# One softmax at the kernel's start: maxima subtracted by a second pass of scores on PE instead of by ACT's bias; one step of a weight decode moved by one

## The chip, the cores and the metric

One core of one Trainium2 chip runs the whole program in one launch. The metric is the device time of one execution in microseconds. Engine names: PE (matrix products), DVE, ACT and POOL (element by element), SP (issues DMAs).

## The reference

Three layers run one after the other, all in float32. The attention has 4 sequences of 576 tokens, 8 heads of 64; heads 0–3 see the last 32 tokens, heads 4–7 every 32nd token:

```
scores = scale * (q @ k.T);  scores = where(mask[head], scores, -1e9)
attn = exp(scores - max(scores));  attn = attn / (sum(attn) + 1e-9)
x = attn @ v                                  # 2304 tokens x 512
h = x @ w_in;   x = (h * cos(h)) @ w_out      # 512 -> 2048 -> 512
h = x @ w_in2;  P = a0 + a1*h + a2*h^2 + a3*h^3
Q = 1 + |b0|*|h| + |b1|*h^2;  out = (P / (Q + 1e-6)) @ w_out2
```

Both layers' weights reach the chip as 64-bit floating-point numbers and are made float32 there; the scale is 1/8.

## The kernel before, in words

**Tiling.** A sequence is worked in two halves of 288 tokens, numbered n = 0 to 7 over the four sequences; the two halves of sequence 0 are n = 0 and n = 1. Heads go in four pairs (0, 1 local; 2, 3 strided). For one half and one pair, five blocks of queries have scores against 89 key columns (local) or, in a second half, 126 columns (strided): 445 columns in one PSUM bank, or 378 and 252 columns in two. PSUM has eight banks: two tagged `a`, two `h`, four `y`.

**The float32 products** of the two dense layers are three products of rounded parts each (high·high, high·low, low·high). So every input (`xh`, `xl`, by `att_oe`, L367: ACT makes the high part, DVE the low part), every activation (`gh`, `gl`) and every weight (`wh`, `wl`) is split in two.

**Stages.** `START` (L82), a list written by hand, is run command by command before the first dense step (L813–814). It holds all of the attention of n = 0, and of n = 1 the scores and the softmax up to the sums, while the first weights are decoded. Then come steps g = 0, 1, ... of the first dense layer, each of which works 128 of the 2048 columns of one block of tokens: `l1` (products into `h`, L408), a gate on ACT, DVE and POOL, and some steps later `l2` (products into `y`, L427). Attention of later halves is strewn in between, by tables. The second dense layer follows after 128 such steps.

**The softmax of n = 1** in `START` takes two commands for each pair. `red` (`att_red`, L289) has DVE reduce the scores in PSUM to the maximum of each row and block (L292) and scale it by −1/8 (L293). `exps` (`att_exps`, L296) has ACT do five exponentials, one for each block, with that maximum as bias (L302), and each adds up its row's sum by an accumulator that is read out by an instruction of its own. Two other forms are in the file: `redn` with `ex` (L317–327), which expects that the maximum has been subtracted in PSUM, and `att_s` (L214) called a second time, which writes the scores again into the same banks and adds a product of the unit matrix with the negative maxima (L249–250).

**What sets the order.** The program's order on each engine is the order in which these commands and steps issue it; no scheduler changes it. An engine runs its own queue in order and waits where an input isn't there or a buffer isn't free. Scores of n = 1 lie in the four `y` banks (pairs 0 to 2) and the two `a` banks (pair 3). On DVE, the reductions of `START` are followed by the decode of weights (L154, L156), the reciprocals of the sums (L333, L334) and the gate of step 0 (L499, L507, L511).

**Second weights.** While the first layer runs, the 32 tiles of the second layer's weights are decoded (`plan_w2`, L579) in 16 slots of two tiles. Each slot of `W2ABS` (L80) names five steps: load, g0, g1, g2, g3. In step g0, `first` has ACT make for each tile the magnitude (L143) and the low bits (L147); in g1, `second` calls `dec_ops` with 0, which does nothing; in g2 DVE merges both (L154); in g3 DVE sets the sign (L156) and the tile is stored. A step's order is a string of letters (`C_ORD`, L86): `N` is the sine (L509), `M` the gate's product (L511), `L` runs what the step has planned of this kind.

Of the kernel before, what the change touches and what calls it, by code (L numbers as in the profile page):

```python
# [91 lines left out]
def attention_moe_moe_kernel(ctx: ExitStack, tc: tile.TileContext, qk0, qk, vv, w1, w2, consts, a, b, out):  # L92
# [42 lines left out]
        (eng or SP).dma_start(out=t.rearrange("p n w -> p (n w)"), in_=src[f, o].bitcast(I32))  # L135
        raws[key, f, o] = t

    def dec_abs(key, f, o, eng=None):
        t = raws.pop((key, f, o))
        m = stage("dec")  # L140
        src = t[:, :, 1].bitcast(F32)
        if eng is None:
            ACT.activation(out=m, in_=src, func=AF.Copy, scale=2.0 ** -112)  # L143
        else:
            eng.tensor_scalar(out=m, in0=src, scalar1=2.0 ** -112, scalar2=None, op0=ALU.mult)

# [770 lines left out]
```

## Time and profile before

| | |
|---|---|
| three runs | 977.61, 979.04, 979.51 us (median 979.04) |
| the profiled execution's own time | 975.9 us |
| its span | 974.1 us, granted PE clock 0.987 on average |
| PE busy | 919.2 us (94%) |
| DVE, ACT, POOL busy | 700.5 (72%), 707.9 (73%), 292.5 us (30%) |
| DMA | 91 GB/s over the span |

PE is busy nearly throughout, but not in the first tenth of the span, where attention and weight decode fill it badly. The profiled execution took 1.8 us more than its span and is 3.1 us shorter than the median of the three runs. A busy time is the time in which an engine's instructions run; an idle time in brackets stands ahead of the instruction that ended it, with the instruction that released it.

### The profile page before, as it was taken

The page shows a single profiled execution, that of the slowest core. Times are in us where ns is not written, and L with a number is a line of the kernel's source. Part 1 is how long each engine was busy: PE and PEld are TensorE (multiplying, and loading weights), DVE is VectorE, ACT ScalarE, POOL GpSimd, SP SyncE. Part 2 cuts the span into 40 slices and gives each one's busy share as a digit, 9 for nine tenths or more (in the row PEclk, how much of TensorE's full clock was granted, in tenths as well). Part 3 has the DMA queues.
Part 4 walks back from the last instruction along what each step waited for, and adds up shares of the span by engine and source line. Part 5 has one row for each costly group of instructions (what it writes and reads, how often), then busy time and mean ns, then how long its engine had stood idle before and what let it go on. Part 6 is the DMA issues. An engine that isn't in the chain of part 4 may idle for free.

```text
span 974.1 us, 17268 instructions
## 1 busy us (share of the span) xinstructions
PE 919.2 (94%) x6367; PEld 857.1 (88%) x6367; DVE 700.5 (72%) x1305; ACT 707.9 (73%) x1485; POOL 292.5 (30%) x279
## 2 busy tenths in 40 slices
PE   7678999999999999999899999999999999999997
PEld 6567999998989989899899978888898898898895
DVE  5997754775555575656658797787787787787776
ACT  5987765665775865757758877777777877777875
POOL 2577722142222132221312223223223223232221
PEclk9799999999999999999999999999999999999999
DMA  9766104435335244344226420010100100100000
GB/s 309 265 221 210 45 2 129 152 112 149 114 101 156 93 144 140 130 136 148 91 78 201 128 78 1 8 58 1 40 26 1 66 1 1 66 1 0 34 1 33
DMA packets 51525, 89.35 MB, mean 92 GB/s; under 512 B 4584, under 2 KB 28400, under 8 KB 51440
## 3 DMA queue, kind: packets, MB, share of 16 engines
q1 hardware_dynamic: 50720, 86.58, 27.0%
q10 hardware_dynamic: 720, 1.67, 0.5%
q8 instruction: 50, 0.82, 0.3%
q14 instruction: 35, 0.29, 0.1%
HBM read 70.40 MB, written 17.83 MB: 91 GB/s over the span
## 4 chain that ended last, share of the span: by engine, by line
PE 23%; ACT 22%; DVE 19%; POOL 10%; issue 5%; DMA 1%; POOLq 0%; ACTq 0%; DVEq 0%
PE h L408 10%; POOL z L467 9%; PE y L427 9%; DVE r L470 7%; ACT r L466 6%; ACT r L465 5%; ACT gh L476 4%; DVE h L471 3%; DVE a L471 3%; PE a L363 1%; PE a L248 1%; DVE t L511 1%; PE a L344 1%; ACT dec L143 1%; ACT L509 1%
## 5 line engine op out<-in xcount | busy, mean ns | idle before, releaser
L408 PE MATMUL h<-xh,w 128*128 128x288 f32 (+3 forms) x1408 | 338.6, 312 | 15.5 <-DVE t L511 11.9
L408 PEld LDWEIGHTS h<-xh,w 128*128 128x128 f32 x1408 | 245.1, 191 | 21.7 <-DVE t L511 13.1
L427 PE MATMUL y<-gh,w 128*128 128x288 f32 (+2 forms) x1024 | 229.3, 300 | 0.5 <-ACT w L162 0.5
L408 PE MATMUL h<-xl,w 128*128 128x288 f32 (+3 forms) x704 | 206.8, 310 | 0.0
L427 PE MATMUL y<-w,gh 128*128 128x512 f32 x576 | 195.9, 393 | 5.6 <-DVE ev L441 4.6
L467 POOL TENSOR_TENSOR z<-q,r 128x384 f32<-128x384 f32 x96 | 97.4, 1014 | 297.9 <-ACT r L466 287.8
L427 PEld LDWEIGHTS y<-gh,w 128*128 128x128 f32 x1024 | 172.1, 189 | 0.8 <-ACT w L162 0.8
L427 PE MATMUL y<-gl,w 128*128 128x288 f32 (+2 forms) x512 | 151.7, 296 | 2.2 <-POOL gl L517 2.1
L408 PEld LDWEIGHTS h<-xl,w 128*128 128x128 f32 x704 | 134.7, 191 | 1.8
L427 PEld LDWEIGHTS y<-w,gh 128*128 128x128 f32 x576 | 108.1, 188 | 28.1 <-DVE ev L441 7.1
L517 POOL TENSOR_TENSOR gl<-t,gh 128x288 fp32r<-128x288 f32 (+2 forms) x67 | 68.6, 1025 | 186.9 <-ACT gh L515 162.0
L470 DVE SCALAR_TENSOR_TENSOR r<-z,r 128x384 f32<-128x384 f32 x96 | 69.5, 724 | 74.1 <-POOL z L467 74.1
L427 PE MATMUL y<-w,gl 128*128 128x512 f32 x288 | 114.7, 398 | 5.2 <-DVE gl L481 5.0
L497 ACT ACTIVATE t<-h,biases 128x288 int32<-128x288 f32 (+2 forms) x116 | 57.7, 497 | 78.5 <-PE h L408 66.1
L507 DVE SCALAR_TENSOR_TENSOR u<-h,t 128x288 f32<-128x288 f32 (+2 forms) x128 | 58.2, 455 | 68.5 <-ACT hs L503 53.3
L408 PE MATMUL a<-xh,w 128*128 128x384 f32 x384 | 106.2, 337 | 0.0
L427 PEld LDWEIGHTS y<-gl,w 128*128 128x128 f32 x512 | 97.1, 190 | 3.0 <-POOL gl L517 2.9
L515 ACT ACTIVATE gh<-t 128x288 fp32r<-128x288 f32 (+2 forms) x128 | 56.7, 443 | 27.7 <-DVE t L511 25.6
L509 ACT ACTIVATE u<-u,biases 128x288 f32<-128x288 f32 (+2 forms) x128 | 67.8, 530 | 12.1 <-DVE u L507 11.7
L511 DVE TENSOR_TENSOR t<-u,hs 128x288 f32<-128x288 f32 (+1 forms) x91 | 49.2, 541 | 36.7 <-ACT u L509 36.5
L408 PEld LDWEIGHTS a<-xh,w 128*128 128x128 f32 x384 | 70.5, 188 | 1.8
L427 PEld LDWEIGHTS y<-w,gl 128*128 128x128 f32 x288 | 54.0, 188 | 20.1 <-DVE gl L481 12.1
(113 smaller groups left out, 1612.9 us busy)
## 6 DMA issues: line engine op xcount, KB each, us to landing
raw<-in_w_dram SPq DMA_DIRECT2D x63, 512.0 KB
qk<-in_qk_dram SPq DMA_DIRECT2D x18, 481.0 KB
wf<-dec SPq DMA_DIRECT2D x32, 256.0 KB
wf<-wf SPq DMA_DIRECT2D x32, 256.0 KB
x2s<-x2d SPq DMA_DIRECT2D x24, 192.0 KB
out_dram<-ev SPq DMA_DIRECT2D x17, 256.0 KB
v<-in_vv_dram SPq DMA_DIRECT2D x16, 240.0 KB
v<-in_vv_dram SPq DMA_DIRECT2D x24, 157.5 KB
```

The source lines that it names most:

```text
L408: PE.matmul(h[:, :n], w[d["ph"], f, 0][:, 128 * c:128 * c + 128], x[c][:, cs], start=k == 0, stop=k == len(ops) - 1)
L427: PE.matmul(y, l, r, start=first and i == 0 and bk != bB, stop=last and i == 2 and bk != bA)
L466: ACT.activation(out=r, in_=r, func=AF.Exp, scale=-1.0, bias=biases[:, 1:2])
L467: POOL.tensor_tensor(out=z, in0=q, in1=r, op=ALU.mult)
L470: DVE.scalar_tensor_tensor(out=r, in0=z, scalar=2.0, in1=r, op0=ALU.subtract, op1=ALU.mult, reverse0=True)
L471: DVE.scalar_tensor_tensor(out=h, in0=h, scalar=ab[:, 0:1], in1=r, op0=ALU.add, op1=ALU.mult)
L497: ACT.activation(out=k, in_=h, func=AF.Identity, scale=INV_2PI, bias=biases[:, 2:3])
L507: DVE.scalar_tensor_tensor(out=u, in0=h, scalar=INV_2PI, in1=k, op0=ALU.mult, op1=ALU.subtract)
L509: ACT.activation(out=u, in_=u, func=AF.Sin, scale=TWO_PI, bias=biases[:, 3:4])
L511: DVE.tensor_tensor(out=t, in0=u, in1=e.get("hs", h), op=ALU.mult)
L515: ACT.activation(out=e["gh"], in_=t, func=AF.Copy)
L517: (POOL if c == "H" else DVE).tensor_tensor(out=e["gl"], in0=t, in1=e["gh"].bitcast(F32), op=ALU.subtract)
```

## The change

In `START`, for n = 1: `oe 0 3` (the split of the last outputs of n = 0) stands ahead of the softmax instead of behind the second `red`. `red` becomes `redn`; then `psub` has PE do the whole score pass of that pair a second time into the same banks (mask, scores, and the product of the unit matrix with the negative maxima, 445 or 378 + 252 columns); `ex` is one exponential for each bank; `sum` is a reduction on DVE. For that the tiles of q and k are kept (a flag that was there). In the second weights' decode, the low bits are made in step g1 instead of g0, by a function `dec_low` cut out of `dec_abs`. The tables are untouched; lines behind `dec_abs` are 4 higher in the new file.

```diff
-START = [ ...
-'s 1 3 a', 'red 1 0', 'd 2 1 2', 'red 1 1', 'd 2 0 2', 'exps 1 0', 'oe 0 3', 'split 2 0 POOL', 'exps 1 1',
-'red 1 2', 'split 2 1 POOL', 'd 3 1 0', 'red 1 3', 'exps 1 2', 'exps 1 3', 'd 3 0 0', 'd 3 0 1', 'd 3 1 1',
...
+START = [ ...
+'s 1 3 a', 'oe 0 3', 'redn 1 0', 'psub 1 0', 'd 2 1 2', 'redn 1 1', 'psub 1 1', 'd 2 0 2', 'ex 1 0', 'sum 1 0',
+'split 2 0 POOL', 'ex 1 1', 'sum 1 1', 'redn 1 2', 'psub 1 2', 'split 2 1 POOL', 'd 3 1 0', 'redn 1 3', 'psub 1 3',
+'ex 1 2', 'sum 1 2', 'ex 1 3', 'sum 1 3', 'd 3 0 0', 'd 3 0 1', 'd 3 1 1',
...
+    def dec_low(t):
+        src = t.rearrange("p n w -> p (n w)").bitcast(U8).rearrange("p (n b) -> p n b", b=8)[:, :, 3]
+        ACT.activation(out=t[:, :, 0], in_=src, func=AF.Copy, scale=1.0 / 32.0, bias=-31.0 / 64.0)
...
-    def dec_abs(key, f, o, eng=None):
+    def dec_abs(key, f, o, eng=None, low=True):
...
-        ACT.activation(out=t[:, :, 0], in_=t.rearrange("p n w -> p (n w)").bitcast(U8).rearrange("p (n b) -> p n b", b=8)[:, :, 3],
-                       func=AF.Copy, scale=1.0 / 32.0, bias=-31.0 / 64.0)
+        if low:
+            dec_low(t)
...
             def first(f=f):
-                raws["m", f] = [dec_abs(2, f, o) for o in range(2)]
+                raws["m", f] = [dec_abs(2, f, o, low=False) for o in range(2)]
...
             def second(f=f, c=0):
                 for t, m in raws["m", f]:
-                    dec_ops(c, t, m)
+                    dec_ops(c, t, m) if c else dec_low(t)
```

On PE, at the end of `START`, the row of before goes from the last scores of n = 1 (pair 3, in the `a` banks) straight to the first products of step 0 (L408):

```order
L237 MATMUL a<-cst_78 128x378
L245 MATMUL a<-k_249,qk 64x126 x6
L237 LDWEIGHTS cst_78
L237 MATMUL a<-cst_78 128x252
L245 MATMUL a<-k_249,qk 64x126 x4
L408 MATMUL h<-xh_84,w_403 128x256
L408 MATMUL h<-xl_88,w_403 128x256
L408 MATMUL h<-xh_85,w_403 128x256
L408 MATMUL h<-xl_89,w_403 128x256
```

Now, behind those scores, the same pass stands once more for each pair, with a product of `mx` at each bank's end, and only then the products of step 0 (L412 now). The rows are those of pair 3's second pass; 16 rows of the same kind, for pairs 0 to 2, stand ahead of them:

```order
L241 LDWEIGHTS cst_78
L241 MATMUL a<-cst_78 128x378
L249 MATMUL a<-k_249,qk 64x126 x6
L254 MATMUL a<-mx,cst 128x378
L241 LDWEIGHTS cst_78
L241 MATMUL a<-cst_78 128x252
L249 MATMUL a<-k_249,qk 64x126 x4
L254 MATMUL a<-mx,cst 128x252
L412 MATMUL h<-xh_84,w_403 128x256
L412 MATMUL h<-xl_88,w_403 128x256
L412 MATMUL h<-xh_85,w_403 128x256
L412 MATMUL h<-xl_89,w_403 128x256
```

So all second passes are ahead of the first `h` in PE's queue.

On DVE, at the same place, before: the last maxima of n = 1 (pair 3's are those of `a`), then the decode of the next weights (L154, L156) and the first reciprocal:

```order
L156 SCALAR_TENSOR_TENSOR dec<-raw,dec 128x512
L375 TENSOR_TENSOR xl_91<-a,xh_87 128x32x9
L292 TENSOR_REDUCE mx<-y 128x3
L292 TENSOR_REDUCE mx<-y 128x2
L293 TENSOR_SCALAR mx<-mx 128x5
L292 TENSOR_REDUCE mx<-a 128x3
L292 TENSOR_REDUCE mx<-a 128x2
L293 TENSOR_SCALAR mx<-mx 128x5
L154 SCALAR_TENSOR_TENSOR dec<-dec,raw 128x512 x2
L156 SCALAR_TENSOR_TENSOR dec<-raw,dec 128x512 x2
L164 CAST w_582<-dec 128x512
L333 TENSOR_SCALAR sm<-sm 128x5
L334 RECIPROCAL sm<-sm 128x5
```

Now with sums (L290) among them; `L324` and `L325` are `redn`, `L158` and `L160` the decode, and the split `xl_91` has gone ahead of the part shown:

```order
L160 SCALAR_TENSOR_TENSOR dec<-raw,dec 128x512
L290 TENSOR_REDUCE sm<-p 128x5 x2
L324 TENSOR_REDUCE mx<-y 128x3
L324 TENSOR_REDUCE mx<-y 128x2
L325 TENSOR_SCALAR mx<-mx 128x5
L324 TENSOR_REDUCE mx<-a 128x3
L324 TENSOR_REDUCE mx<-a 128x2
L325 TENSOR_SCALAR mx<-mx 128x5
L290 TENSOR_REDUCE sm<-p 128x5 x2
L158 SCALAR_TENSOR_TENSOR dec<-dec,raw 128x512 x2
L160 SCALAR_TENSOR_TENSOR dec<-raw,dec 128x512 x2
L168 CAST w_624<-dec 128x512
```

The sums of pairs 0 and 1 now stand ahead of the maxima of pairs 2 and 3, and the sums of pairs 2 and 3 ahead of the decode (L158) and of all that follows it; behind that, DVE's order is as before.

On ACT, in steps 55 and 56 of the first layer (a slot of the second weights with g0 = 55 and g1 = 56), before: magnitude (L143) and low bits (L147) of both tiles in a row, then the sine of step 56 (the second `u`, L509):

```order
L509 ACT_TABLE_LOAD
L509 ACTIVATE u<-u,biases 128x288
L497 ACTIVATE t<-h,biases 128x288
L515 ACTIVATE gh<-t 128x288
L143 ACTIVATE dec<-raw 128x512
L147 ACTIVATE raw<-raw 128x512
L143 ACTIVATE dec<-raw 128x512
L147 ACTIVATE raw<-raw 128x512
L509 ACTIVATE u<-u,biases 128x288
L497 ACTIVATE t<-h,biases 128x288
L503 ACTIVATE hs<-h 128x288
L515 ACTIVATE gh<-t 128x288
```

Now both low bits (L141, of `dec_low`) come behind that sine, in step 56:

```order
L513 ACT_TABLE_LOAD
L513 ACTIVATE u<-u,biases 128x288
L501 ACTIVATE t<-h,biases 128x288
L519 ACTIVATE gh<-t 128x288
L148 ACTIVATE dec<-raw 128x512 x2
L513 ACTIVATE u<-u,biases 128x288
L141 ACTIVATE raw<-raw 128x512 x2
L501 ACTIVATE t<-h,biases 128x288
L507 ACTIVATE hs<-h 128x288
L519 ACTIVATE gh<-t 128x288
```

The orders of POOL and SP are unchanged.

## Rows read from the trace of the kernel before

**Rows 1.** Busy time by stage: window, length, then each engine, clock, DMA.

```profile
core 0: us, PE busy (x) PEld busy (x) DVE busy (x) ACT busy (x) POOL busy (x), PEclk, DMA share, GB/s
...
25.00:50.00 25.00, 15.54 (x133) 13.11 (x128) 23.89 (x39) 24.41 (x73) 13.72 (x12) 0.73 0.73 249
...
90.00:170.00 80.00, 79.29 (x703) 77.81 (x702) 47.76 (x102) 53.31 (x111) 34.35 (x35) 0.98 0.20 61
```

**Rows 2.** Timeline of PE (start, length, engine, line, operation, [idle before <-releaser]), 25–46 us.

```profile
25.33 0.36 PE L237 MATMUL y<-msk,cst 128*128 128x445 bf16 x1
...
28.39 0.33 PE L237 MATMUL a<-cst 128*128 128x378 bf16 x1
...
33.27 0.39 PE L237 MATMUL a<-cst 128*128 128x252 bf16 x1 [2.08 <-DVE xl L375]
...
34.62 0.58 PE L408 MATMUL h<-xh,w 128*128 128x256 f32 x1
...
44.97 0.58 PE L408 MATMUL h<-xh,w 128*128 128x256 f32 x1 [5.83 <-DVE t L511]
```

**Rows 3.** Timeline of DVE, 32–45 us.

```profile
32.56 0.65 DVE L375 TENSOR_TENSOR xl<-a,xh 128x288 fp32r<-128x288 f32 x1 [0.39 <-ACT xh L374]
...
33.12 0.87 DVE L292 TENSOR_REDUCE mx<-y 128x3 f32<-128x378 f32 x2
...
36.35 1.28 DVE L154 SCALAR_TENSOR_TENSOR dec<-dec,raw 128x512 int32<-128x512 int32 x2
...
44.50 0.41 DVE L511 TENSOR_TENSOR t<-u,h 128x256 f32<-128x256 f32 x1
```

**Rows 4.** Timeline of ACT, 11–32 us.

```profile
11.57 0.58 ACT L281 ACTIVATE p<-p 128x445 f32<-128x445 f32 x1 [1.70 <-DVE p L315]
...
30.28 0.34 ACT L302 ACTIVATE p<-y,mx 128x89 f32<-128x89 f32 x1
...
31.85 0.68 ACT L374 ACTIVATE xh<-a 128x288 fp32r<-128x288 f32 x1
```

**Rows 5.** Timeline of PE about a maskless score product, 104–106 us.

```profile
104.24 1.24 PE L248 MATMUL a<-qk 128*128 128x89 f32 x10
...
105.27 0.36 PE L427 MATMUL y<-gh,w 128*128 128x256 f32 x1
```

**Rows 6.** Timeline of DVE: two softmax sums of later sequences.

```profile
138.92 0.61 DVE L286 TENSOR_REDUCE sm<-p 128x5 f32<-128x445 f32 x1
...
217.17 0.80 DVE L286 TENSOR_REDUCE sm<-p 128x5 f32<-128x630 f32 x1
```

**Rows 7.** Busy time and granted clock in two stretches.

```profile
34.60:37.80 3.20, 3.20 (x17) 3.18 (x16) 3.17 (x6) 3.20 (x18) 1.28 (x1) 0.50 1.03 408
...
37.80:39.00 1.20, 1.20 (x11) 1.13 (x10) 1.17 (x3) 1.20 (x7) 0.00 (x0) 1.00 1.00 396
```

**Rows 8.** What PE waited for, 150–560 us: total, times, longest (us).

```profile
PE h L408 <- DVE t L511: 4.3, 2, 2.2
PE a L344 <- POOL p L335: 2.9, 2, 1.5
PE h L408 <- DVE u L507: 2.6, 3, 0.9
PE a L363 <- ACT pt L352: 1.4, 1, 1.4
```

**Rows 9.** Timeline of ACT, 271–274 us.

```profile
271.05 0.66 ACT L143 ACTIVATE dec<-raw 128x512 f32<-128x512 f32 x1
...
273.26 0.52 ACT L509 ACTIVATE u<-u,biases 128x288 f32<-128x288 f32 x1
```

**Rows 10.** Timeline of DVE at three steps that decode second weights.

```profile
207.13 0.53 DVE L511 TENSOR_TENSOR t<-u,hs 128x352 f32<-128x352 f32 x1 [2.63 <-ACT u L509]
...
273.40 0.69 DVE L154 SCALAR_TENSOR_TENSOR dec<-dec,raw 128x512 int32<-128x512 int32 x1 [0.40 <-ACT raw L147]
...
339.33 0.46 DVE L511 TENSOR_TENSOR t<-u,hs 128x288 f32<-128x288 f32 x1 [2.41 <-ACT u L509]
```

More of the change, by code (lines that the diff above doesn't have):

```diff
@@ L81 @@
 BLAG = 8
-START = ['cst ACT', 'lq 0 0', 'lq 0 2 ACT', 'load 2 0', 'lv 0 1', 'lv 0 3 w0', 'lq 0 3', 'lq 0 1 ACT', 'load 0 0', 'lv 0 0', 'load 0 1', 'load 1 0 ACT', 'load 1 1', 'warm 38', 'lv 0 2 w0', 'masks', 's 0 0 y', 's 0 1 y', 's 0 2 y', 's 0 3 y', 'lq 1 0', 'ab', 'lq 1 2', 'lq 1 1', 'load 2 1', 'load 3 0', 'load 3 1', 'red 0 0', 'lv 1 0', 'exps 0 0', 'lq 1 3', 'ms 0 1', 'ex 0 1', 'red 0 2', 'lv 1 1', 'exps 0 2', 'norm 0 0 POOL', 'ms 0 3', 'ex 0 3', 'load 4 1', 'sum 0 1', 'norm 0 2 POOL', 'norm 0 1 POOL', 'sum 0 3', 'warm 29', 'abs 0 0', 'abs 0 1', 't 0 0 h', 'load 4 0', 'te 0 0', 'd 0 0 0', 'norm 0 3 POOL', 'o 0 0', 'd 0 1 0', 'd 0 0 1', 'd 0 1 1', 'd 0 0 2', 'd 0 1 2', 't 0 1 y', 'abs 1 1', 'te 0 1', 'oe 0 0', 'split 0 1 POOL', 'abs 1 0', 't 0 2 h', 'o 0 1', 'd 1 1 0', 'd 1 1 1', 'd 1 0 0', 'te 0 2', 'load 6 1', 'd 1 0 1', 'split 0 0 POOL', 'd 1 0 2', 't 0 3 y', 'oe 0 1', 's 1 0 y', 'te 0 3', 'd 1 1 2', 'o 0 2', 'split 1 0 POOL', 'oe 0 2', 'split 1 1 POOL', 'o 0 3', 's 1 1 y', 'abs 2 0', 'abs 2 1 DVE', 'd 2 0 0', 'd 2 1 0', 'abs 3 0', 'd 2 0 1', 'd 2 1 1', 'abs 3 1', 's 1 2 y', 's 1 3 a', 'red 1 0', 'd 2 1 2', 'red 1 1', 'd 2 0 2', 'exps 1 0', 'oe 0 3', 'split 2 0 POOL', 'exps 1 1', 'red 1 2', 'split 2 1 POOL', 'd 3 1 0', 'red 1 3', 'exps 1 2', 'exps 1 3', 'd 3 0 0', 'd 3 0 1', 'd 3 1 1', 'd 3 0 2', 'd 3 1 2', 'split 3 0 POOL', 'load 5 0', 'load 5 1', 'load 7 0', 'split 3 1 POOL DVE', 'load 7 1', 'load 6 0', 'next']
@@ new lines @@
+START = ['cst ACT', 'lq 0 0', 'lq 0 2 ACT', 'load 2 0', 'lv 0 1', 'lv 0 3 w0', 'lq 0 3', 'lq 0 1 ACT', 'load 0 0', 'lv 0 0', 'load 0 1', 'load 1 0 ACT', 'load 1 1', 'warm 38', 'lv 0 2 w0', 'masks', 's 0 0 y', 's 0 1 y', 's 0 2 y', 's 0 3 y', 'lq 1 0', 'ab', 'lq 1 2', 'lq 1 1', 'load 2 1', 'load 3 0', 'load 3 1', 'red 0 0', 'lv 1 0', 'exps 0 0', 'lq 1 3', 'ms 0 1', 'ex 0 1', 'red 0 2', 'lv 1 1', 'exps 0 2', 'norm 0 0 POOL', 'ms 0 3', 'ex 0 3', 'load 4 1', 'sum 0 1', 'norm 0 2 POOL', 'norm 0 1 POOL', 'sum 0 3', 'warm 29', 'abs 0 0', 'abs 0 1', 't 0 0 h', 'load 4 0', 'te 0 0', 'd 0 0 0', 'norm 0 3 POOL', 'o 0 0', 'd 0 1 0', 'd 0 0 1', 'd 0 1 1', 'd 0 0 2', 'd 0 1 2', 't 0 1 y', 'abs 1 1', 'te 0 1', 'oe 0 0', 'split 0 1 POOL', 'abs 1 0', 't 0 2 h', 'o 0 1', 'd 1 1 0', 'd 1 1 1', 'd 1 0 0', 'te 0 2', 'load 6 1', 'd 1 0 1', 'split 0 0 POOL', 'd 1 0 2', 't 0 3 y', 'oe 0 1', 's 1 0 y', 'te 0 3', 'd 1 1 2', 'o 0 2', 'split 1 0 POOL', 'oe 0 2', 'split 1 1 POOL', 'o 0 3', 's 1 1 y', 'abs 2 0', 'abs 2 1 DVE', 'd 2 0 0', 'd 2 1 0', 'abs 3 0', 'd 2 0 1', 'd 2 1 1', 'abs 3 1', 's 1 2 y', 's 1 3 a', 'oe 0 3', 'redn 1 0', 'psub 1 0', 'd 2 1 2', 'redn 1 1', 'psub 1 1', 'd 2 0 2', 'ex 1 0', 'sum 1 0', 'split 2 0 POOL', 'ex 1 1', 'sum 1 1', 'redn 1 2', 'psub 1 2', 'split 2 1 POOL', 'd 3 1 0', 'redn 1 3', 'psub 1 3', 'ex 1 2', 'sum 1 2', 'ex 1 3', 'sum 1 3', 'd 3 0 0', 'd 3 0 1', 'd 3 1 1', 'd 3 0 2', 'd 3 1 2', 'split 3 0 POOL', 'load 5 0', 'load 5 1', 'load 7 0', 'split 3 1 POOL DVE', 'load 7 1', 'load 6 0', 'next']
```

## The prediction

> **What bounds the kernel now.** I began with the busy times by stage. From 90 us on PE hardly rests (79.29 of 80 us in 90–170), but in 25–50 us PE is busy only 15.54 of 25 us, while DVE is busy 23.89 and ACT 24.41 [rows 1]. So the end of `START` is bound by DVE and ACT, and what is added to their chains there moves all that follows.
>
> The timelines say what that chain is. PE ends the last scores of n = 1 at 34.62 us and does one step's products; then it waits 5.83 us, until 44.97, for the gate's product on DVE (L511, 44.50) [rows 2, 3]. DVE has no gap longer than 0.39 us ahead of that: it takes the last split, the maxima of pairs 2 and 3 (from 33.12), and at 36.35 the decode (L154), with which the work of the steps begins [rows 3]. ACT's queue goes on from that decode's results, too: the high part of those weights (L162) can only follow it. So one number carries most of the forecast: when that L154 starts.
>
> Third, the waits of PE in the first layer, for the second edit: from 150 to 560 us PE waited 4.3 us in 2 waits for L511, 2.6 for L507, 2.9 in 2 for normalised probabilities (L335) and 1.4 for L352 [rows 8]. All of these are late results of the engines on which the decode of the second weights also runs.
>
> **Edit 1, the second pass of scores (+11.3 us).** Removed: 20 small exponentials and 20 accumulator reads on ACT, 1.57 us a pair for the local ones (30.28 to 31.85) [rows 4]. DVE only swaps a factor. Added: four exponentials over whole banks, four sums on DVE, a second pass on PE. Counted as busy time, this would be near zero; what matters is the order. The maxima of pair 2 may be taken only after DVE's sums of pairs 0 and 1, which need their exponentials, which need the second pass; the second pass of pair 2 overwrites the bank that this maximum reads, so it can't begin before; and the decode stands behind the sums of pairs 2 and 3. What ran side by side becomes one chain: all of PE's second pass, plus two breaks in which PE waits. Step by step:
>
> - Start. The split of pair 3's inputs no longer waits for pair 0's exponentials: it starts at 30.28 instead of 31.85 [rows 4], 1.57 us earlier, and so do the last scores, which waited for it [2.08 us, rows 2]. PE has done them at 34.62 − 1.57 = 33.05.
> - Scores and masks again. Two pairs (1 and 2) took 28.39 − 25.33 = 3.06 us [rows 2]; pairs 0 and 3 have the same shapes as these, so four take 6.12.
> - Products with the maxima, 445 + 445 + 630 + 630 = 2150 columns. None such is in the trace. From above: a maskless product of five blocks of 89 columns took 105.27 − 104.24 = 1.03 us [rows 5], or 2.3 ns a column: 4.98. From below: a mask pass of 445 columns in a shorter type took 0.36 [rows 2]: 1.74. I take 3.9, nearer to the upper row, which is of the same type and the same 128 rows.
> - The middle break: one exponential of 445 columns (0.58) [rows 4], one sum (0.61) [rows 6], the first reduction of pair 2 (about 0.5, half of the 0.87 with its follower and a little for the scaling) [rows 3], and 0.1 to hand over: 1.8.
> - The end break: two exponentials of pair 3 (378 and 252 columns, about 0.9 by the 0.58 for 445), one sum of 630 columns (0.80) [rows 6], 0.1: 1.8.
>
> 33.05 + 6.12 + 3.9 + 3.6 = 46.67, against 36.35: +10.3. Those durations are at the full clock. PE's clock was 0.50 (1.2 GHz) until 37.8 and 1.00 (2.4 GHz) after it [rows 7]; in the second pass PE works after just such idle time. If half of pair 0's second pass (about 2.0 us at full clock) runs at 1.2 GHz, 1.0 is added: **+11.3**. With the lower price of the maxima +8.1 at the full clock; with pairs 0 and 1 all at 1.2 GHz (4.0 more) +14.3; with everything at 1.2 GHz (10 more) about +20.
>
> The Trainium skill ("TensorE: Matmul & The Clock Gate", "What's actually happening") says that the throttled state is the default and that activity releases it. By that the earlier work of the second pass could bring the clock up earlier than 37.8, and the sum would be +10.3; were the rise tied to the moment at which it came before, most of pair 0's and 1's pass would run at half, and it would be about +12.3. The row of before shows only that the clock rose while PE worked without rest, which speaks for the rule and does not settle it.
>
> Does the shift last? Behind L154 DVE's order is as before, ACT's next work waits for it, and PE's `h` products, behind the second pass, wait for the gate on DVE. POOL works on their results. So everything behind is moved rigidly. PE's wait of 5.83 us [rows 2] doesn't absorb it, since its releaser moves as well. The only cover would be loads (the DMA share is 0.73 in 25–50 [rows 1]), but none of the stretch's longest waits ends on one. ACT is freed of the 40 small instructions, yet waits for DVE, so this is worth nothing.
>
> **Edit 2, low bits one step later (−2.3 us).** In the step g0 ACT does four decode operations in a row ahead of the next sine: 271.05 to 273.26, 2.21 us [rows 9]; two remain, so that the sine comes 1.1 earlier, and the other two come behind it in g1. Over 16 slots most of this lies under PE's work, except where PE waits for the gate's chain:
>
> - The waits for L507 and L352 at 200 and 223 us. DVE waited 2.63 us for the sine at 207.13 [rows 10] and worked without rest until the second of them. I take 0.95 gained of both.
> - The waits for L335 and L507 in steps around 337–347, and again one period of 32 steps (129.3 us) later: DVE waited 2.41 us for the sine at 339.33 [rows 10]. 1.15 each, close to what the sine gains: 2.3.
> - The two waits for L511 (274.5 and 403.8 us). There the decode's `L` stands ahead of `M`, and DVE's L154 already waits for the low bits (0.40 at 273.40) [rows 10]. They will be made after the sine instead of ahead of it, so that L154 and the gate's product behind it come later: I put 0.45 each, 0.9 lost.
>
> −0.95 − 2.3 + 0.9 ≈ −2.3. Bounds: if all the waits named that can gain go, 2.9 + 2.6 + 1.4 = −6.9 [rows 8]; if none gains, and the low bits delay ACT in g1 by as much as the sine gained once more, +2.0.
>
> **Sum.** 975.9 + 11.3 − 2.3 = 984.9 for a profiled execution. That one is 3.1 under the median of the runs, 979.04, so I predict 979.04 + 9.0 = 988.0.
>
> **Rivals.**
> - *Cheap products with the maxima* (at the lower bound): edit 1 costs 8.1, and the median is 979.04 + 8.1 − 2.3 = 984.8. For it: PE's one long product (a whole bank) has no change of weights in between. Against: the nearest row of the type is 2.3 ns a column.
> - *The clock stays at 1.2 GHz throughout the second pass*, since PE stops at the middle break: edit 1 costs 18 to 20, and the median is 995 to 997. For it: it was at half until 37.8 in spite of the work ahead of that [rows 7]. Against: PE was busy throughout 34.6–37.8, and the clock rose behind it [rows 7]; in the second pass of pairs 0 and 1 PE has no break either.
> - *The low bits gain nothing*: they come in front of DVE's merge instead of in front of the sine, and only the 0.9 is left; 979.04 + 11.3 + 0.9 = 991.2. For it: DVE's L154 already waited for L147 twice. Against: the waits of 2.41 and 2.63 for the sine.
> - *Faster*: the start's shift vanishes in PE's waits of 39–90 us (5.83 the longest), as ACT is relieved and its chain sets the pace there, and edit 2's −2.3 remains: 976.7. It decides if ACT, not DVE, sets when step 0's gate runs. For it: ACT is busier than DVE, 24.41 against 23.89 [rows 1]. Against: the decode on DVE stands behind the last sum in DVE's own queue, and ACT's part needs it.
>
> **How the numbers follow.** Forecast (984–990.5) 0.50, cheap products 0.20, half clock 0.10, no gain from edit 2 0.14, faster 0.06. Faster and slower are told from the same at 0.2% of 979.04, 977.1 to 981.0, which is about what a measurement of this kernel can tell. All but the last case lie above 981, though the cheap products with edit 2 at its best (−6.9) come to 980.2; so same 0.04, faster 0.05, slower 0.91. The range 982.8 to 994.8 takes in the cheap products and the case without a gain from edit 2, and leaves out most of the half clock and of the faster case.
>
> **What would show it.** The first L154 of the steps (L158 now) at about 47.6 instead of 36.35, with the split of pair 3 near 30.3; PE idle about 1.8 us between the second passes of pairs 1 and 2, and once more after pair 3's; the products at L254 near 0.8 us for 445 columns; the clock at 1.2 GHz in the first second pass only; the products of step 1 at about 56 instead of 44.97. Behind 90 us everything is shifted by one amount, which then shrinks at 200–223, 337–347 and 466–476 us by about 1 each, and grows by about 0.45 at 274 and 404. The prediction is wrong if PE's second passes run beside other reductions without the breaks, if the shift at 90 us is well under 8, or if the waits for L507 and L335 stay as they were.

## The result, and the profile after

The changed kernel takes 989.98 us (median of 4 runs, 988.46 to 992.01) against 978.84 for the kernel before in the same comparison (4 runs): the ratio is 1.0125 with a 95% interval of 1.0111 to 1.0139. It is slower, by 11.1 us of the medians. Its profiled execution took 989.55 us (span 987.8), 13.65 more than the profiled execution before.

**The end of START.** The stretch that answers to the first row of [rows 1], with the same columns:

```profile
25.00:50.00 25.00, 20.80 (x234) 14.01 (x230) 13.11 (x25) 10.59 (x21) 6.41 (x5) 0.93 0.72 250
```

PE has gone from 15.54 to 20.80 us of work there, DVE from 23.89 to 13.11 and ACT from 24.41 to 10.59. The two engines that were full now wait. Work was taken off both of them, and the program became longer: busy time was not what this stretch paid for.

PE's timeline (start, length, engine, line, operation, [idle before <-releaser]), which answers to [rows 2]:

```profile
34.24 0.36 PE L241 MATMUL y<-msk,cst 128*128 128x445 bf16 x1
...
36.16 1.85 PE L254 MATMUL y<-mx,cst 128*128 128x445 f32 x2
...
39.12 1.01 PE L254 MATMUL y<-mx,cst 128*128 128x445 f32 x2
...
41.94 0.32 PE L241 MATMUL y<-cst 128*128 128x378 bf16 x1 [1.81 <-DVE mx L324]
...
42.99 0.90 PE L254 MATMUL y<-mx,cst 128*128 128x378 f32 x2
43.73 0.27 PE L241 MATMUL y<-cst 128*128 128x252 bf16 x1
...
47.60 0.69 PE L254 MATMUL a<-mx,cst 128*128 128x252 f32 x2
47.95 0.46 PE L412 MATMUL h<-xh,w 128*128 128x256 f32 x1
...
58.16 0.58 PE L412 MATMUL h<-xh,w 128*128 128x256 f32 x1 [7.03 <-DVE t L515]
```

DVE's timeline, which answers to [rows 3]:

```profile
32.76 0.64 DVE L379 TENSOR_TENSOR xl<-a,xh 128x288 fp32r<-128x288 f32 x1 [1.55 <-ACT xh L378]
...
38.69 0.62 DVE L290 TENSOR_REDUCE sm<-p 128x5 f32<-128x445 f32 x1 [2.63 <-ACT p L331]
...
41.35 0.87 DVE L324 TENSOR_REDUCE mx<-y 128x3 f32<-128x378 f32 x2
...
48.82 0.81 DVE L290 TENSOR_REDUCE sm<-p 128x5 f32<-128x630 f32 x1 [2.29 <-ACT p L331]
...
49.54 1.28 DVE L158 SCALAR_TENSOR_TENSOR dec<-dec,raw 128x512 int32<-128x512 int32 x2
...
57.70 0.41 DVE L515 TENSOR_TENSOR t<-u,h 128x256 f32<-128x256 f32 x1
```

The chain can be read across both. PE begins the second pass at 34.24, behind the last scores. The product with the maxima takes 1.85 us for pair 0 and 1.01 for pair 1 (L254). DVE waits 2.63 us for pair 0's exponentials before its first sum (38.69), and takes pair 2's maximum (41.35) only behind two sums. PE waits 1.81 us for that maximum (41.94). Then come pairs 2 and 3, the last exponential, DVE's last sum (48.82, after 2.29 us of waiting), and only then, at 49.54, the decode (L158), which started at 36.35 before. Behind pair 3's second pass PE goes straight on with the products of steps 0 and 1 (from 47.95). Those of step 2 (58.16) wait 7.03 us for the gate's product at 57.70; before, they started at 44.97.

ACT's split of pair 3, for [rows 4]:

```profile
32.05 0.68 ACT L378 ACTIVATE xh<-a 128x288 fp32r<-128x288 f32 x1
```

The granted clock, with the columns of the first block above, in three stretches of the changed kernel:

```profile
18.00:24.50 6.50, 6.35 (x56) 5.40 (x56) 3.94 (x7) 5.57 (x14) 1.70 (x2) 0.51 1.02 357
...
34.30:37.70 3.40, 3.40 (x24) 2.10 (x24) 1.72 (x4) 0.00 (x0) 0.00 (x0) 0.55 1.04 412
...
38.00:50.00 12.00, 10.19 (x92) 6.82 (x91) 5.32 (x11) 3.86 (x8) 2.53 (x2) 1.00 0.36 143
```

and in the first of these stretches in the kernel before:

```profile
18.00:24.50 6.50, 5.28 (x96) 4.47 (x96) 5.03 (x9) 6.50 (x17) 2.71 (x3) 1.00 1.04 363
```

PE was at 1.2 GHz (0.5) for the second pass of pair 0 and at 2.4 GHz for the rest of it. It was also at 1.2 GHz in 18–24.5, where the two programs are still the same and PE was at 2.4 GHz in the profile before. That is no effect of the change. In this execution ACT's split of pair 3 starts at 32.05 instead of the 30.28 that was expected; in e1, with the same `START` and the clock at 1.00 in that stretch, it starts at 29.88. So part of the 13.65 us between the two profiles is chance.

**The first layer.** PE's waits in 150–560 us, which answer to [rows 8] (total, times, longest):

```profile
PE h L412 <- DVE t L515: 6.4, 2, 3.2
PE h L412 <- DVE u L511: 2.6, 3, 0.9
PE a L348 <- POOL p L339: 1.6, 2, 0.8
PE a L367 <- ACT pt L356: 0.4, 1, 0.4
```

The waits for L339 went from 2.9 to 1.6 us and those for L356 from 1.4 to 0.4. Those for L511 (L507 before) stayed at 2.6, and those for the gate's product (L515) went from 4.3 to 6.4. In steps 55 to 57, ACT:

```profile
282.72 1.21 ACT L148 ACTIVATE dec<-raw 128x512 f32<-128x512 f32 x2
...
283.83 0.52 ACT L513 ACTIVATE u<-u,biases 128x288 f32<-128x288 f32 x1
...
284.26 1.20 ACT L141 ACTIVATE raw<-raw 128x512 int32<-128x512 uint8 x2
```

and DVE's merge with what stands behind it:

```profile
284.93 1.29 DVE L158 SCALAR_TENSOR_TENSOR dec<-dec,raw 128x512 int32<-128x512 int32 x2 [1.62 <-ACT raw L141]
...
286.14 0.45 DVE L515 TENSOR_TENSOR t<-u,h 128x288 f32<-128x288 f32 x1
```

The same gate's product before:

```profile
274.00 0.45 DVE L511 TENSOR_TENSOR t<-u,h 128x288 f32<-128x288 f32 x1
```

and the first product of steps 57 and 58 on PE:

```profile
286.64 0.40 PE L412 MATMUL h<-xh,w 128*128 128x288 f32 x1 [3.24 <-DVE t L515]
...
291.45 0.29 PE L412 MATMUL h<-xh,w 128*128 128x288 f32 x1
```

The sine (L513) now starts behind two decode operations, but the two low bits (L141) come right behind it, and DVE's merge waits 1.62 us for the first of them. The gate's product follows at 286.14, and PE has waited 3.24 us instead of 2.19. The next step then took 291.45 − 286.64 = 4.81 us instead of 3.28. The clock tells why; the same columns, behind this wait and behind that of step 89:

```profile
287.40:290.40 3.00, 3.00 (x14) 3.00 (x13) 0.80 (x2) 1.00 (x4) 0.60 (x1) 0.50 0.00 0
...
418.00:421.00 3.00, 3.00 (x17) 3.00 (x16) 0.75 (x1) 0.62 (x2) 0.76 (x1) 0.61 0.02 5
```

The first product of a step in both profiles, worked out from the timelines, shows where the difference was gained and lost:

```
step        before    after    shift
   0         34.62    47.95    13.33
   2         44.97    58.16    13.19
  44        216.61   228.95    12.34   (as from step 30 on)
  46        228.95   240.04    11.09
  56        269.00   280.08    11.08
  57        274.50   286.64    12.14
  58        277.78   291.45    13.67
  73        336.97   350.49    13.52
  76        350.23   362.70    12.47
  88        398.33   410.89    12.56
  89        403.75   417.41    13.66
  90        407.02   421.99    14.97
 105        466.17   481.05    14.88
 110        488.82   502.53    13.71
 223        956.57   970.20    13.63
```

Three gains (1.25 at 45–46, 1.0 at 74–76 and 1.2 at 106–110) stand against two losses (2.6 at 57–58 and 2.4 at 89–90). The second layer keeps the shift as it is.

### The profile page after: what moved, and what is told of

Read it like the earlier page. It is cut to its first block, busy times and chain, and to the rows that moved or that the text cites. A ratio compares the mean times of both kernels' runs of the same rounds, so it can differ in the third digit from the quotient of the medians.

```text
span 987.8 us, 17433 instructions
## 1 busy us (share of the span) xinstructions
PE 930.0 (94%) x6465; PEld 864.0 (87%) x6465; DVE 702.4 (71%) x1309; ACT 704.2 (71%) x1451; POOL 290.9 (29%) x279
## 4 chain that ended last, share of the span: by engine, by line
PE 23%; ACT 22%; DVE 17%; POOL 10%; issue 5%; DMA 1%; POOLq 0%; ACTq 0%
PE h L412 10%; POOL z L471 9%; PE y L431 9%; DVE r L474 7%; ACT r L470 6%; ACT r L469 5%; ACT gh L480 4%; DVE h L475 3%; DVE a L475 3%; PE a L367 1%; PE a L252 1%; ACT L285 1%; PE a L348 1%; DVE t L515 1%; ACT L513 1%
## 5 line engine op out<-in xcount | busy, mean ns | idle before, releaser
L412 PE MATMUL h<-xh,w 128*128 128x288 f32 (+3 forms) x1408 | 337.8, 312 | 19.1 <-DVE t L515 15.8
L412 PEld LDWEIGHTS h<-xh,w 128*128 128x128 f32 x1408 | 244.4, 190 | 24.6 <-DVE t L515 16.9
L412 PE MATMUL h<-xl,w 128*128 128x288 f32 (+3 forms) x704 | 206.2, 309 | 0.0
L412 PEld LDWEIGHTS h<-xl,w 128*128 128x128 f32 x704 | 134.0, 190 | 1.9
L521 POOL TENSOR_TENSOR gl<-t,gh 128x288 fp32r<-128x288 f32 (+2 forms) x67 | 66.0, 986 | 185.9 <-ACT gh L519 162.4
L511 DVE SCALAR_TENSOR_TENSOR u<-h,t 128x288 f32<-128x288 f32 (+2 forms) x128 | 58.2, 454 | 76.8 <-ACT hs L507 62.2
L412 PE MATMUL a<-xh,w 128*128 128x384 f32 x384 | 106.2, 337 | 0.0
L513 ACT ACTIVATE u<-u,biases 128x288 f32<-128x288 f32 (+2 forms) x128 | 67.7, 529 | 11.7 <-DVE u L511 11.5
L515 DVE TENSOR_TENSOR t<-u,hs 128x288 f32<-128x288 f32 (+1 forms) x91 | 50.5, 555 | 33.0 <-ACT u L513 32.5
L412 PEld LDWEIGHTS a<-xh,w 128*128 128x128 f32 x384 | 70.5, 188 | 1.9
```

The costliest lines, as they stand in the source:

```text
L412: PE.matmul(h[:, :n], w[d["ph"], f, 0][:, 128 * c:128 * c + 128], x[c][:, cs], start=k == 0, stop=k == len(ops) - 1)
L511: DVE.scalar_tensor_tensor(out=u, in0=h, scalar=INV_2PI, in1=k, op0=ALU.mult, op1=ALU.subtract)
L513: ACT.activation(out=u, in_=u, func=AF.Sin, scale=TWO_PI, bias=biases[:, 3:4])
L515: DVE.tensor_tensor(out=t, in0=u, in1=e.get("hs", h), op=ALU.mult)
L521: (POOL if c == "H" else DVE).tensor_tensor(out=e["gl"], in0=t, in1=e["gh"].bitcast(F32), op=ALU.subtract)
```

## The experiments

Two theories stood against each other. Theory 1: `START` costs nearly all of the loss, and the low bits' gains are given back in steps 57 and 89, by a longer wait and by PE's slower clock behind it. Theory 2: the low bits gain what was predicted, and `START` costs more. Times are medians; each comparison has runs of the kernel before on the same chip.

**e1, START alone.**

```diff
-                raws["m", f] = [dec_abs(2, f, o, low=False) for o in range(2)]
+                raws["m", f] = [dec_abs(2, f, o) for o in range(2)]
...
-                    dec_ops(c, t, m) if c else dec_low(t)
+                    dec_ops(c, t, m)
```

> The kernel before with the new START alone (second pass of scores, maxima as products, sums on DVE); the low bits stay in step g0. Theory 1 (from the two traces: the START change is worth nearly all of the loss, and the low bits net to about +0.4): 10.5 to 11 us over the kernel before, about 989.5; the first decode behind START starts 10 to 13 us later than 36.35; no PE clock drop near 287 and 417 us. Theory 2 (the prediction's: the low bits gain 2.3, so the START change costs all of 13.4): about 992.

Measured: 989.23 against 978.45, ratio 1.0109 (1.0090 to 1.0127), so 10.7 us (8.8 to 12.4). DVE, the split of pair 3 and the decode behind `START`:

```profile
30.54 0.65 DVE L375 TENSOR_TENSOR xl<-a,xh 128x288 fp32r<-128x288 f32 x1 [1.44 <-ACT xh L374]
...
48.69 1.28 DVE L154 SCALAR_TENSOR_TENSOR dec<-dec,raw 128x512 int32<-128x512 int32 x2
```

From the split to the decode it is 18.15 us here (16.78 in the changed kernel; here the last scores ran at 1.2 GHz as well), against 3.79 before [rows 3]. Theory 1 holds for the size. One expectation failed: the clock did fall behind step 89's wait (a shift of +1.48 at step 90), though its length was only 2.1 us.

**e2, the low bits alone** (the changed kernel with the old `START` list).

> The kernel before with the low bits of the second weights in step g1 alone; START is the old one. Theory 1: gains of about 1 us each in the waits at 223, 340 to 350 and 470 to 480 us (3.7 in all) and a loss of about 2.5 each at 274.5 and 403.8 us (1.1 of longer wait for the gate's product and 1.4 because PE's clock falls to 1.2 GHz just behind the wait), net -0.5 to +1.5, about 979.2. Theory 2 (the prediction's sizes): -2.3, 976.5. Rival: without the START change the wait at 274.5 stays short of the length at which the clock fell, and the net is about -1.5.

Measured: 979.83 against 978.45, ratio 1.0006 (0.9992 to 1.0020): no gain. The interval excludes the predicted −2.3. In its trace the two losses are 1.05 + 1.35 and 1.14 + 1.51 us, with waits of 3.2 us and the clock at 1.2 GHz behind both: theory 1.

**e3, the low bits in all slots but those two.**

```diff
-                raws["m", f] = [dec_abs(2, f, o, low=False) for o in range(2)]
+                raws["m", f] = [dec_abs(2, f, o, low=slots[f][2] in (56, 88)) for o in range(2)]
...
             def second(f=f, c=0):
+                if c == 0 and slots[f][2] in (56, 88):
+                    return
```

> As the low bits alone, but the two slots with g1 = 56 and 88, in which the merge on DVE stands ahead of the gate's product, keep their low bits in g0. Theory 1 (the loss is in these two slots): the gains stay and the losses go, 3 to 4 us under the kernel before, about 975.3, waits of 2.2 at 274 and 404 as before, no clock drop there. Rival (the losses are the gains given back by the same chain elsewhere): no better than the low bits in all 16 slots.

Measured: 977.12 against 978.45, ratio 0.9991 (0.9979 to 1.0004): no change that can be told. A miss. The waits at steps 57 and 89 were 2.8 us, not 2.2 (a shift of +0.6 and +0.7), and the clock fell behind both (+1.3 and +1.5). The trace shows where the 0.6 comes from. ACT before, at a load of its table for the exponential:

```profile
258.70 1.28 ACT L281 ACT_TABLE_LOAD   x1
```

and here, with what stands ahead of it:

```profile
255.38 0.50 ACT L501 ACTIVATE t<-h,biases 128x288 int32<-128x288 f32 x1 [0.47 <-PE h L412]
...
256.41 1.23 ACT L141 ACTIVATE raw<-raw 128x512 int32<-128x512 uint8 x2
257.66 1.28 ACT L285 ACT_TABLE_LOAD   x1
```

PE comes 1.64 us earlier here than before at steps 46 to 56, but ACT's load only 1.04. In between lies another slot, that with g1 = 52, whose low bits had moved: ACT, which no longer makes them in step 51, waits 0.47 us for PE's `h` and makes them behind it (L141). So ACT comes 0.6 late by PE's time, is still so at the decode of step 55, and the gate's product of step 56 with it. In the changed kernel the decode of step 55 is late by the same 0.6 (282.72 against 271.05 [rows 9], 11.67, where PE's shift is 11.08). No run kept the low bits of that slot alone in g0.

**e4, the merge moved behind the gate's product as well.**

```diff
-24: 'swNLMUKjVGHT'
+24: 'swNMUKjVGHTL'
```

> The low bits in g1 in all 16 slots, and in steps 56, 88 and 120 the letter L (which issues decode and softmax work) stands at the end of the step's order instead of ahead of the gate's product M. Theory 1 (the gate's product of steps 56 and 88 is late only because DVE's merge waits for the low bits ahead of it): the product comes 1 to 1.5 us earlier than in the kernel before, PE's waits at 274 and 404 shrink from 2.2 to about 1, no clock drop; with the other gains 5 to 6 us under the kernel before, about 973.5. Rival: the softmax work that L also issues (sums, reciprocals) comes too late behind, PE waits for probabilities (L335) or transposes instead, and the time is 976 to 979.

Measured: 972.40 against 978.45, ratio 0.9932 (0.9915 to 0.9948), 6.6 us faster than the kernel before. DVE's gate product of step 56 now waits for the sine only, and PE's waits for it:

```profile
274.70 0.45 DVE L515 TENSOR_TENSOR t<-u,h 128x288 f32<-128x288 f32 x1 [1.07 <-ACT u L513]
```

```profile
PE h L412 <- DVE t L515: 3.0, 2, 1.5
```

3.0 us in two waits, against 6.4 in the changed kernel; the clock stays up behind both (1.00, and no step behind them is longer). So the low bits do have a gain; with the letter `L` ahead of `M` it was lost at these two places.

**e8, that letter alone** (low bits in g0 as before).

> The kernel before with the low bits in g0 as they were, and only the letter L of steps 56, 88 and 120 moved to the end of the order. Theory 1 (the sine behind four decode operations holds the gate's product there; L only adds its wait): 0.3 to 0.6 gained at each of the two waits, about 977.5, so that the 6 us of e4 come from both edits together. Rival (e4's gain is that of L alone): 974 to 975.

Measured: 979.33 against 979.44, ratio 1.0004 (0.9992 to 1.0016). Alone, the letter brings no gain that can be told; its two waits are 3.9 us together instead of 4.3. Only both edits bring the 6.6 us: first the sine must come earlier, then the product must be allowed to follow it. But PE was at 1.2 GHz behind both waits in this trace, too (columns as above):

```profile
276.50:279.50 3.00, 3.00 (x15) 3.00 (x14) 2.09 (x3) 1.19 (x4) 1.16 (x1) 0.50 0.03 8
...
406.00:409.00 3.00, 3.00 (x14) 3.00 (x14) 2.58 (x4) 0.79 (x3) 1.29 (x1) 0.50 0.00 0
```

**e7, PE kept at work during the two waits** (the low bits alone, and this).

```diff
+                if g in (57, 89):
+                    wait = bank("a")
+                    for _ in range(24):
+                        PE.matmul(wait[:, :2 * WL], msk16[:, 0:128], msk16, start=True, stop=True)
                 h = l1(bk, f)
```

> The low bits in g1 alone (as e2) with 24 small products (bfloat16, 178 columns, about 2.7 us, their result unused) in PE's queue ahead of the products of steps 57 and 89, so that PE works during the two waits for the gate. Theory 1 (1.3 to 1.5 of the loss at each place is PE at 1.2 GHz behind the wait): no clock drop there, step 57 takes 3.3 us instead of 4.8, 2.6 to 3 us under e2's time, the longer release (1.0 each) stays; about 977. Rival (the slow products have another cause, a weight or activation that comes late): as e2, 979.8.

Measured: 976.30 against 979.44, ratio 0.9972 (0.9960 to 0.9985); e2 was at 1.0006. The unused products and the first product of steps 57 and 58:

```profile
271.18 2.01 PE L661 MATMUL a<-msk 128*128 128x178 bf16 x24
...
274.61 0.40 PE L412 MATMUL h<-xh,w 128*128 128x288 f32 x1 [1.42 <-DVE t L515]
...
277.89 0.29 PE L412 MATMUL h<-xh,w 128*128 128x288 f32 x1
```

PE still waits until 274.61, but step 57 takes 3.28 us again. The slow products behind the wait were the clock's doing; theory 1.

**e9, the same unused products in the kernel before.**

> The kernel before, with the 24 small unused products ahead of the products of steps 57 and 89 as in e7. Theory 1 (the clock falls behind the wait of 2 us in most executions of the kernel before, too, and its profiled execution, 975.9, was one in which it didn't): 1.5 to 3 us under the kernel before, 976 to 977.5, and with it the low bits alone on the same footing (e7) are within 1.5 us of it. Rival (the kernel before keeps its clock there, and only the longer wait of the change loses it): the same as before, 979.

Measured: 976.76 against 977.81, ratio 0.9984 (0.9975 to 0.9993), 1.6 us (0.7 to 2.4). So the kernel before loses time to the clock there as well; its first profile shows that it does not always.

**e10, the kernel before once more, for another profile.**

> The kernel before once more, unchanged, for one more profile. Theory 1: PE's clock falls to 1.2 GHz for a stretch behind the waits of 2.2 us at about 275 and 404 us, each step behind it 1.5 us longer than in the first profile; time 978 to 981. Rival: no fall there, and the time differs from 975.9 by START alone.

Measured: 978.22. The clock behind the two waits, of 2.2 and 2.1 us:

```profile
275.00:278.00 3.00, 2.14 (x16) 2.14 (x17) 1.89 (x4) 1.99 (x6) 0.81 (x1) 1.00 0.03 8
...
404.80:407.80 3.00, 3.00 (x13) 3.00 (x14) 0.84 (x2) 0.73 (x2) 0.80 (x1) 0.50 0.00 0
```

At the first place it stayed, at the second it fell and cost 1.54 us: between theory 1 and its rival. The last step comes 2.3 us later here than in the first profile, and 1.54 of that is this fall: 975.9 was an execution in which both places went well.

**e5, the same START instructions, sums last.**

```diff
-'oe 0 3', 'redn 1 0', 'psub 1 0', 'd 2 1 2', 'redn 1 1', 'psub 1 1', 'd 2 0 2', 'ex 1 0', 'sum 1 0', ...
+'oe 0 3', 'redn 1 0', 'psub 1 0', 'd 2 1 2', 'redn 1 1', 'psub 1 1', 'd 2 0 2', 'redn 1 2', 'psub 1 2', 'redn 1 3', 'psub 1 3', 'ex 1 0', ...
+'load 7 1', 'load 6 0', 'sum 1 0', 'sum 1 1', 'sum 1 2', 'sum 1 3', 'next'
```

> The new START alone, with its commands in another order: all four maxima (redn) first, then all second passes, and DVE's four sums behind the decode of the next weights (at the end of START) instead of among the maxima. The same instructions as in the START change alone (+10.8), so if busy time or the clock were the cost, the time stays about 989. Theory 1 (the cost is the chain maximum - second pass - exponential - sum - next maximum, with the decode behind it): PE's middle break of 1.8 us goes, the decode on DVE starts near 36.5 again, and what is late is step 0's products behind the second passes (about 48.5 for the first gate operation instead of 41.8); 5 to 7.5 us over the kernel before, about 984.5.

Measured: 985.22 against 979.44, ratio 1.0068 (1.0049 to 1.0088), 6.7 us. DVE, the split of pair 3, the decode, the last sum and the gate of step 0; and PE's first product of step 0:

```profile
32.45 0.64 DVE L375 TENSOR_TENSOR xl<-a,xh 128x288 fp32r<-128x288 f32 x1 [1.53 <-ACT xh L374]
...
38.04 1.29 DVE L154 SCALAR_TENSOR_TENSOR dec<-dec,raw 128x512 int32<-128x512 int32 x2 [0.32 <-issue]
...
46.46 0.81 DVE L286 TENSOR_REDUCE sm<-p 128x5 f32<-128x630 f32 x1 [1.68 <-ACT p L327]
...
49.73 0.38 DVE L499 TENSOR_SCALAR t<-h 128x256 int32<-128x256 f32 x1
```

```profile
45.66 0.47 PE L408 MATMUL h<-xh,w 128*128 128x256 f32 x1
```

From the split to the decode it is 5.6 us instead of 16.8, and PE's middle break is gone. With the same instructions, 4 of the 10.7 us went by order alone. What stays is a chain, too: the gate (49.73) comes well behind PE's product of step 0 (45.66), since it stands in DVE's queue behind the last sum, which waits 1.68 us for the last exponential of pair 3 and so for PE's second passes. What the added work alone would cost, no run shows.

**e6, the new way for pairs 0 and 1 only.**

```diff
-'sum 1 1', 'redn 1 2', 'psub 1 2', 'split 2 1 POOL', 'd 3 1 0', 'redn 1 3', 'psub 1 3', 'ex 1 2', 'sum 1 2', 'ex 1 3', 'sum 1 3',
+'sum 1 1', 'red 1 2', 'split 2 1 POOL', 'd 3 1 0', 'red 1 3', 'exps 1 2', 'exps 1 3',
```

> The new START alone, but pairs 2 and 3 go the old way (maximum scaled, five exponentials with bias each on ACT, no second pass, no sum on DVE); pairs 0 and 1 the new way. Theory 1: the second pass of pairs 2 and 3 (5.7 us with its products) and the end break go, ACT's ten small exponentials with read-outs (3.4 us) come back behind the middle break: the decode starts about 5.5 to 6.5 us later than in the kernel before; about 985. Rival (each pair costs alike): half of 10.8, 983.8 - not told apart by time, but by the trace: DVE's decode at about 42.5, PE's step 0 products ahead of it.

Measured: 986.09 against 979.44, ratio 1.0079 (1.0063 to 1.0094), 7.7 us (6.2 to 9.2), somewhat over the expected 5.5 to 6.5. DVE's split and decode, and ACT's first operation behind its small exponentials:

```profile
33.29 0.64 DVE L375 TENSOR_TENSOR xl<-a,xh 128x288 fp32r<-128x288 f32 x1 [1.53 <-ACT xh L374]
...
44.00 1.29 DVE L154 SCALAR_TENSOR_TENSOR dec<-dec,raw 128x512 int32<-128x512 int32 x2
```

```profile
46.57 0.67 ACT L162 ACTIVATE w<-dec 128x512 fp32r<-128x512 f32 x1
```

The decode comes 10.7 us behind the split; but ACT's high part (L162) starts only at 46.57, 2.6 us behind the decode instead of the 1.9 of before, since the small exponentials now follow the middle break instead of filling the time ahead of it. Four equal shares would make half of e1's loss, 5.4 us (4.4 to 6.2), which is under the 7.7; so the first two pairs seem to cost more than half, though the two ranges touch.

**e11, e4 with one command of the new START.**

```diff
-'red 1 0', 'd 2 1 2', 'red 1 1', 'd 2 0 2', 'exps 1 0', 'oe 0 3', 'split 2 0 POOL', 'exps 1 1',
+'oe 0 3', 'red 1 0', 'd 2 1 2', 'red 1 1', 'd 2 0 2', 'exps 1 0', 'split 2 0 POOL', 'exps 1 1',
```

> e4 (low bits in g1, L at the end of steps 56, 88 and 120, old softmax) and the one command of the new START that adds nothing: oe 0 3 ahead of the softmax of n = 1. The split of pair 3 starts 1.57 us earlier, but DVE had no idle time left there above 0.4: 972.0, at most 1 us under e4. Rival: ACT's first exponentials come 0.7 later and with them the decode behind them: 973.

Measured: 973.58 against 977.81, ratio 0.9959 (0.9946 to 0.9971): faster than the kernel before, but 2.7 thousandths less so than e4 by the ratios. DVE's split of pair 3 and the decode:

```profile
32.09 0.64 DVE L379 TENSOR_TENSOR xl<-a,xh 128x288 fp32r<-128x288 f32 x1 [1.52 <-ACT xh L378]
...
39.43 1.28 DVE L158 SCALAR_TENSOR_TENSOR dec<-dec,raw 128x512 int32<-128x512 int32 x2
```

7.34 us lie between them instead of 3.79, for the maxima of pairs 0 and 1 no longer fill the time in which DVE waits for the split. Neither expectation had this. e4 stays the best version that ran.

## Why the prediction was right, and which term was not

- **The direction, the place and the size as a whole** were right: 988.0 was predicted and 989.98 measured, inside the range. That it came so near is in part luck, since steps of edit 1 were off in both directions, and edit 2 brought no gain.
- **Edit 1 (+11.3).** Measured alone 10.7 (8.8 to 12.4). The chain was named rightly. From ACT's split of pair 3 to the decode it took 17.49 us (32.05 to 49.54); the prediction's steps make 17.39 (30.28 to 46.67, and 1.0 for the clock). PE's middle break was 1.81 (predicted 1.8). The other steps cancel: the last scores took 2.19 (32.05 to 34.24) instead of 2.77, the four second passes 12.24 (34.24 to 48.29 without the break) instead of 11.02, and from PE's last product (47.60 + 0.69) to the decode it was 1.25 instead of 1.8. Behind pair 3's pass PE did not have the second break that the prediction expected: it had steps 0 and 1 to do. (Before, too, PE did two steps' products ahead of its wait and not one; the products at 44.97, put down to step 1, are step 2's.) The products with the maxima took 0.74 us from start to start for 378 columns (42.99 to 43.73), or 2.0 ns a column, between the 1.8 that was taken and the 2.3 of the row from above. The clock was half for pair 0's second pass alone, nearly the case that was taken: 3.56 us, against 2.33 for pair 1's. The Trainium skill ("TensorE: Matmul & The Clock Gate", "What's actually happening") lets activity release the throttle; the trace agrees in that the clock rose within the second pass (0.55 in 34.3–37.7, 1.00 in 38–50), though this was no earlier than the 37.8 of before. From DVE's split to the decode 16.78 against 3.79 is +12.99; less the 1.57 that the split gains, 11.4. That gain is not seen in this profile, with the slower clock at 18–24.5, but in e1 (30.54 against 32.56 [rows 3]).
- **Edit 2 (−2.3) failed**: measured alone it is +0.6 (−0.8 to +2.0). Its gains came, 1.25 where 0.95 was predicted, and 1.0 and 1.2 where 1.15 was predicted for each. The waits that shrank are those for L352 and L335; those for L507, on which the prediction had put part of the gain, stayed at 2.6 us. The term "I put 0.45 each, 0.9 lost" was right in what it described. Counted from the start of ACT's decode in step 55, the sine came 1.1 earlier (1.11 us behind it instead of 2.21), and the gate's product 0.47 later. For that product comes 12.14 later than before (286.14 against 274.00), the decode 11.67. What failed is the step "most of this lies under PE's work, except where PE waits for the gate's chain". At each of the two places ACT's queue came 0.6 late from the slot before (e3), which was put at nothing, and so PE's wait grew by 1.05 and 1.10 instead of 0.45. And the price of a longer wait was left out: PE's clock fell behind it, 1.3 to 1.5 us more at each place. e7 shows it, which keeps PE at work there (ratio 0.9972 against e2's 1.0006, 3.3 us), and e4, which takes most of the wait away. With the clock kept up in both kernels, e7 against e9, the low bits alone are worth 0.9972 against 0.9984, about −1.2 us, as the gains of 3.5 and the longer waits of 2.2 leave; the two intervals overlap, so by time this is not shown.
- **The two profiles.** The 3.1 us by which the profiled execution stood under the median was taken as an offset that both kernels share. e9 and e10 show that a part of it was the clock at the very place of edit 2: the kernel before pays for it in some executions, and with the low bits moved in all slots and the order kept it was paid at both places in both profiles (the changed kernel, e2). So part of the loss of edit 2 was already in the kernel before's median.
- **The rivals.** The low bits without a gain (14%) came nearest: 991.2 was its time, though the gains came and were lost again elsewhere. Cheap products and the half clock throughout fell by the rows above. The shift was not absorbed: 13.33 at step 0, still 12.34 at step 44 and 13.63 at the end.

What stays open: why PE's clock was at 1.2 GHz in most of 18–24.5 in some executions (0.50 to 0.57 in the changed kernel, e2, e4, e5, e6, e8 and e9), in part of it in others (0.62 to 0.74 in e7, e10 and e11) and not at all in the rest (1.00 in the first of before, e1 and e3), though this part of `START` is the same in all. The waits in front of it, for loads and ACT, differ in each; no run changed them one at a time.

## What to carry to other kernels

When an edit moves work from two full engines to one that waits, draw the new chain before adding up busy time: here 24 us of full engines became 13 and 11, and the program got 10.7 us longer, 4 of which went by another order of the same commands. When work is moved from one step to the next, look also at the steps around it: the queue that was freed may have to wait and then be late. A wait of PE has a price beyond its length where the clock falls behind it; it belongs into the sum as a separate term, and an execution in which it didn't fall is a lucky baseline. And two edits that each bring nothing can be worth 6.6 us together, when one makes an input earlier and the other lets the consumer follow it.

## What the runs showed of the hardware

Behind the waits of steps 57 and 89 PE's clock fell as follows, counted over the two places in each profile without the unused products: of the waits of 1.5 us (e4, e11) none of four, of those of 1.9 to 2.2 us (before, e1, e5, e6, e8, e10) seven of twelve, of those of 2.8 to 3.3 us (the changed kernel, e2, e3) six of six. A fall cost 1.3 to 1.55 us in the step behind it. That the same kernel showed both in one execution (e1, e5, e10) had not been expected; there the wait of 2.2 us kept the clock and that of 2.1 lost it, while in e6 both waits of 2.2 lost it.
